# Attention and two MoE layers on one core: a four-operation weight decoder, diagonals and sums moved to other engines, a split transpose, loads in thirds, and a 32-byte filler

## The chip, the core and the metric

The kernel runs on one core of a Trainium2 chip. The metric is the device time of one execution in microseconds (us); the number before the change is the median of three runs. One further execution was recorded by the hardware profiler, and every row below comes from it. The engines are named as in the profile: PE is the tensor engine's matmul stream, PEld its weight loads, DVE the vector engine, ACT the scalar engine, POOL the GpSimd engine, SP the engine whose queue issues the DMAs.

## The reference

The three stages follow one another, in fp32 (the inputs are 4 x 8 x 576 x 64 for q, k and v; the weights w1, w2 and w3, w_out of the MoE layers have 512 x 768, 768 x 512, 512 x 2048 and 2048 x 512 elements):

```python
scores = q @ k.T / 8 + bias            # bias[h] = relu(log1p(|i-j|)/log1p(max(i,1)) * w1 + b1) @ w2
attn = exp(scores - max(scores)); attn = attn / (sum(attn) + 1e-9)
x = attn @ v                           # to 2304 tokens x 512
h = max(x @ m.w1, x @ m.w2, x @ m.w3)  # 2304 x 768, relu included through the maxima
x = h @ m.w_out                        # 2304 x 512
g = elu(x @ m2.w_in)                   # 2304 x 2048
out = g @ m2.w_out                     # 2304 x 512
```

The weights of the MoE layers arrive as float64 bits (two int32 words for each number) and are turned into float32 on the chip. Both MoE layers compute in a split form: a number is a high part in fp32r plus a low part in fp32r, so that each product takes three matmuls (high by high, high by low, low by high).

## The kernel before

**Prologue (0 to 56 us).** The bias table of all heads is computed with matmuls and written to scratch tiles `scr` in memory. Its last writes end in the first steps of the attention.

**Attention (56 to about 343 us).** There are 16 head pairs n, each with 5 query blocks c, so 80 steps s. Blocks 0 to 3 have 128 queries and both heads; block 4 holds the 64 queries that are left of both heads in one tile, so it has one of everything where the others have two ("one-head step"). A step does this: `unit_qk` (L222, PE) writes the scores of a head into PB[h]; `scores` (L230, DVE) adds the bias tile b_t, scales, stores e_t in SBUF and takes the row minimum; `expo` (L235, ACT) takes the exponential with its sum; `recip` (L240 and L241, DVE) makes 1/(sum + 1e-9); `diag` (L249, POOL, one operation for each head) multiplies a 64 x 64 identity by it, to dg_t; `trans` (L252, PE) multiplies 64 x 64 blocks of e_t by that diagonal into TQ, which transposes and normalises them; `tails` (L252 too, with output pb) does so for the last 64 keys, into columns of PB; `evac` and `evac_tails` (helper lines L75 on ACT, L77 on DVE) copy TQ and the tails to p; `pv` (L319, L323, L327, PE) multiplies by v into the two banks XO[0] and XO[1]. After blocks 1 and 4, `x_copy` (L341, ACT) copies XO[0] to xf, `x_sum` (L345, DVE) adds XO[1], and `x_hi` (L73) and `x_lo` (L81) on POOL split the result into the token tiles xh and xl, which hold all 2304 tokens.

The order in each engine's queue is written by hand: every piece has a key `s + OFF[name]`, and the pieces are issued in order of the key. OFF = qk0 0.0, qk1 0.01, t0 (`scores` of head 0) 0.02, t1 0.03, pump 0.32, ns (`recip`) 1.025, tr 2.10, tl 2.20, evt 2.311, ev0 2.385, ev1 2.387: step s computes scores, while the transposes are those of step s-2. Between t0 and t1 of a step the DVE thus runs the `recip` of the step before. PB[0] is written by `tails` and read by `scores` of head 0: the tails at 2.20 of step s-2 come after t0 of step s, and have to wait until it has read PB[0]. TQ and XO are of two banks each and PB is of two, so no step has a second set.

One `pump` in each step of four out of five runs a piece of the weight decoder (`decoder`, L420 to L430): DVE masks the exponent, ACT changes its bias (L422, with the constant tile `rebias`), DVE shifts and masks, twice combines, and merges (five DVE operations of 512 columns for a tile of 128 x 512 weights). 56 tiles are decoded in all, 14 of them in the attention. Then the split (ACT and POOL) and a store to memory. `load_kq` (L96) fetches q and k of the next pair (864 KB in one DMA), `load_v` (L100) its v, `fetch` (L371) raw weights, `load_b` (L109, L114) the bias tiles after each four pairs; all through SP's queue.

**First MoE layer (343 to 626 us)**: L526 is the matmul of `moe1_mm` (1296 of 128 x 128 by 384 columns, the moving operand being xh or xl), L620 that of `moe1_out` (432 of 384 columns, moving hh or hl). **Second (626 to 1008 us)**: L696 is that of `prod` (1020 of 384 columns, moving xh, xl or the sums tt), L740 that of `moe2_out` (864 of 512 columns, moving the weight tiles w_t, with gh or gl as weights). 94 matmuls of the first layer run already in the last steps of the attention.

**Addresses.** Within a partition every tile of these two layers and of the attention begins 32 bytes past a multiple of 64 (w_t at 17056, xh at 155360, xl at 192224, gh at 41632, hh at 107680), because the tile `rebias` of 4 bytes takes up 32 bytes ahead of them on the left side, and on the right side ident2 and the token tiles add up so. The blocks that a matmul streams are at multiples of 1536 or 512 bytes within the tiles, so each moving row begins 32 bytes past a multiple of 64 as well.

## Time and profile before

| what | value |
|---|---|
| median of three runs | 1013.38 us (1012.16 to 1016.56) |
| the profiled execution's own time | 1010.22 us |
| its span on the core | 1008.4 us |
| mean granted clock of PE | 0.997 of full speed |
| busy: PE, PEld, DVE, ACT, POOL | 977.4, 869.2, 692.1, 526.1, 341.7 us |
| share of PE in the chain of work that ended last | 91% |
| memory traffic | 150.78 MB read, 48.37 MB written |

The profile is read by stages here, since the stages have different limits: a mean over the span hides that PE has idle time in the attention only. The busy time of PE includes time in which a matmul is drawn out by its neighbours, so a row of the timeline gives the start and the drawn-out length of a group of instructions, and the distance between starts is what counts.

### The profile page before, as it was taken

How to read it: one execution, taken by the hardware profiler on the slowest of the kernel's cores; microseconds unless marked ns; L12 is line 12 of the kernel's file. 1: busy time of each engine (PE TensorE's matmuls, PEld its weight loads, DVE VectorE, ACT ScalarE, POOL GpSimd, SP SyncE). 2: the span in 40 equal slices, each digit the busy share in tenths (PEclk: the TensorE clock that was granted, in tenths of full speed). 3: DMA queues.
4: the chain of work that ended last, by engine and by line, in shares of the span. 5: the costliest groups of instructions: out<-in, count | busy, mean ns of one | idle time of the engine just before them, and what ended most of it. 6: DMA issues, size and time to landing. Idle time of an engine off the chain costs nothing.

```text
span 1008.4 us, 28525 instructions
## 1 busy us (share of the span) xinstructions
PE 977.4 (97%) x11748; PEld 869.2 (86%) x11748; DVE 692.1 (69%) x1428; ACT 526.1 (52%) x1087; POOL 341.7 (34%) x419
## 2 busy tenths in 40 slices
PE   7979899999999999999999999999999999999998
PEld 4447777778887899999999999998998989988996
DVE  7967778788886699887887862835574355743342
ACT  8967777777775233333333331644445344453443
POOL 0013344344343354534553550323232132321222
PEclk9989999999999999999999999999999999999999
DMA  7842724645532356879886981355657556575553
GB/s 259 291 172 85 247 94 157 205 163 187 176 127 79 134 187 215 308 234 341 321 282 236 328 298 47 116 189 175 199 192 252 191 171 204 188 258 185 176 197 105
DMA packets 65905, 201.00 MB, mean 199 GB/s; under 512 B 7024, under 2 KB 14832, under 8 KB 65776
## 3 DMA queue, kind: packets, MB, share of 16 engines
q1 hardware_dynamic: 65776, 199.18, 57.6%
q8 instruction: 93, 1.52, 0.6%
q14 instruction: 36, 0.29, 0.1%
HBM read 150.78 MB, written 48.37 MB: 197 GB/s over the span
## 4 chain that ended last, share of the span: by engine, by line
PE 91%; DVE 6%; issue 1%; DMA 1%; ACT 0%; SPq 0%; POOL 0%; DVEq 0%; POOLq 0%; ACTq 0%
PE xo L696 18%; PE pb L740 13%; PE pb L526 12%; PE tq L740 6%; PE tq L252 6%; PE xo L319 6%; PE xo L526 5%; PE tq L526 5%; PE pb L222 5%; PE pb L620 4%; PE pb L183 3%; PE pbb L183 2%; DVE e_t L230 2%; PE xo L620 2%; PE tq L620 2%
## 5 line engine op out<-in xcount | busy, mean ns | idle before, releaser
L81 POOL TENSOR_TENSOR gl<-t_t,gh 128x384 fp32r<-128x384 f32 x96 | 108.7, 1142 | 286.3 <-ACT gh L75 286.3
L235 ACT ACTIVATE e_t<-e_t,st_t 128x576 f32<-128x576 f32 x144 | 111.4, 773 | 58.6 <-DVE st_t L240 56.1
L230 DVE CUSTOM_DVE_ANT_0 e_t<-pb,b_t 128x576 f32<-128x576 f32 x144 | 107.7, 749 | 32.7 <-PE pb L222 32.5
L249 POOL TENSOR_SCALAR dg_t<-ident,st_t 128x64 f32<-128x64 f32 x144 | 48.1, 348 | 212.7 <-DVE st_t L241 93.2
L740 PE MATMUL pb<-w_t,gh 128*128 128x512 f32 x384 | 119.3, 392 | 0.0
L526 PE MATMUL pb<-xh,w_t 128*128 128x384 f32 x448 | 116.8, 336 | 0.0
L252 PEld LDWEIGHTS tq<-dg_t,e_t 64*64 64x64 f32 x4608 | 96.6, 136 | 22.7 <-issue 7.7
L252 PE MATMUL tq<-dg_t,e_t 64*64 64x64 f32 x4608 | 97.8, 222 | 10.9 <-issue 5.3
L696 PE MATMUL xo<-tt,w_t 128*128 128x384 f32 x528 | 107.4, 338 | 0.0
L718 ACT ACTIVATE t_t<-c_t 128x384 f32<-128x384 f32 x96 | 50.0, 521 | 103.4 <-DVE c_t L709 95.6
L222 PE MATMUL pb<-kq_t 64*64 64x288 f32 x1152 | 98.6, 413 | 3.8 <-issue 1.3
L696 PEld LDWEIGHTS xo<-tt,w_t 128*128 128x128 f32 x528 | 95.0, 188 | 7.7 <-issue 0.3
L696 PE MATMUL xo<-xh,w_t 128*128 128x384 f32 x328 | 94.6, 335 | 0.0
L319 PE MATMUL xo<-p,tv_t 64*64 64x320 f32 (+1 forms) x1024 | 85.4, 408 | 1.6 <-issue 1.2
L526 PEld LDWEIGHTS pb<-xh,w_t 128*128 128x128 f32 x448 | 81.1, 188 | 0.5 <-issue 0.4
L740 PEld LDWEIGHTS pb<-w_t,gh 128*128 128x128 f32 x384 | 70.5, 188 | 6.6
L740 PE MATMUL pb<-w_t,gl 128*128 128x512 f32 x192 | 75.5, 393 | 0.0
L526 PE MATMUL pb<-xl,w_t 128*128 128x384 f32 x224 | 75.3, 336 | 0.0
L75 ACT ACTIVATE p<-tq 128x512 f32<-128x512 f32 (+1 forms) x128 | 62.8, 528 | 16.4 <-PE tq L252 15.2
L222 PEld LDWEIGHTS pb<-kq_t 64*64 64x64 f32 x1152 | 50.9, 133 | 22.9 <-DVE p L77 4.4
L75 ACT ACTIVATE gh<-t_t 128x384 fp32r<-128x384 f32 x96 | 48.6, 519 | 33.4 <-DVE t_t L726 33.4
L696 PEld LDWEIGHTS xo<-xh,w_t 128*128 128x128 f32 x328 | 60.2, 188 | 3.0
(131 smaller groups left out, 2198.1 us busy)
## 6 DMA issues: line engine op xcount, KB each, us to landing
w_t<-scw_w SPq DMA_DIRECT2D x90, 512.0 KB, 4.4
w_t<-scw_wi SPq DMA_DIRECT2D x74, 512.0 KB, 4.2
kq_t<-tkq SPq DMA_DIRECT2D x16, 864.0 KB, 5.4
scw_wi<-sp SPq DMA_DIRECT2D x26, 512.0 KB, 4.7
scw_w<-sp SPq DMA_DIRECT2D x22, 512.0 KB, 5.5
raw<-wo SPq DMA_DIRECT2D x22, 512.0 KB, 3.7
scr<-o_t SPq DMA_DIRECT2D x36, 288.0 KB, 3.9
raw<-wm SPq DMA_DIRECT2D x18, 512.0 KB, 4.1
```

Source lines behind the costliest of these rows:

```text
L75: nc.scalar.activation(dst, src, AF.Copy)
L81: e.tensor_tensor(out=dst, in0=src, in1=hi.bitcast(F32), op=ALU.subtract)
L183: mm(p[32 * a4:32 * a4 + 32, 224 + 288 * hf:512 + 288 * hf], w28, FT[A, a4][:, 288 * hf:288 * hf + 288], start=True, stop=True)
L222: mm(PB[h][H64[g], 224 + 288 * r:512 + 288 * r], t[H64[r], 576 + 576 * a + q0:640 + 576 * a + q0], t[H64[r], 288 * a:288 * a + 288], start ...
L230: nc.vector.tensor_tensor_reduce(out=E[s][:, 576 * h:576 * h + 576], in0=PB[h][:, 224:800], in1=BT[n // 4, c, h], op0=ALU.add, op1=ALU.min ...
L235: nc.scalar.activation(e, e, AF.Exp, bias=st[:, h:h + 1], scale=-1.0, accum_out=st[:, 2 + h:3 + h])
L252: mm(dst, E[s][H64[g], k0:k0 + 64], DG[s][H64[g], h % nheads(s)], start=True, stop=True)
L319: mm(XO[g][H64[h], 0:w], v[H64[g], 128 * k + 64 * h:128 * k + 64 * h + 64], ps[0][H64[g], 4 * h + k, :], start=(k == 0), stop=(k == 3 and ...
L526: mm(ps[blk][:, 0:NB], wt[:, ks], xt[:, kk, t0:t0 + NB], start=(j == 0), stop=(j == 11))
L620: mm(ps[blk][:, 0:NB], WO[0][:, kk, wt, ms], xt[:, bs], start=(j == 0), stop=(j == 3 * NM1 - 1))
L696: mm(ps, w[wt][:, ks], b[xt][:, kk], start=(start and j == 0), stop=(stop and j == 5), skip_group_check=True)
L740: mm(acc[t], g[:, ts], w[k], start=(f == 0 and i == 0 and j == 0), stop=(f == NU - 1 and i == 1 and j == 2))
```

## The change

- **Decoder.** `magnitude` takes the absolute value of the high words as floats on ACT, one tile ahead; DVE then clamps it (max and min with two constants), shifts it left by three, and merges sign and low bits in two operations: four DVE operations instead of five, the number of pumps for a tile stays five. The tile `rebias` is gone.
- **Diagonals.** One DVE operation for both heads (L247 of the new file), right behind the reciprocal, in place of one or two on POOL.
- **Sums.** ACT copies both banks of XO to two tiles xf; POOL adds them.
- **Evacuation.** EVD has 3 beside 0 and 2: in block 3 the second half of TQ is copied by DVE and no longer by ACT.
- **Transposes.** `trans` is called for one head at a time, and the tails come between the two.
- **Loads.** q and k of the next pair come as three DMAs of 288 KB, at steps 1.2, 2.2 and 3.2 of a pair instead of one at 0.2; v one step later.
- **Addresses.** A tile of 32 bytes, `align`, is reserved beside xh and xl. With it and without `rebias` all the tiles named above begin at a multiple of 64 (w_t 17024, xh 155328, xl 192192, gh 41600, hh 107648). The tiles of the prologue stay where they were.

```diff
-OFF = {"qk0": 0.0, "qk1": 0.01, "t0": 0.02, "ns": 1.025, "dg": 1.026, "t1": 0.03, "tr": 2.10, "tl": 2.20, "evt": 2.311,
+OFF = {"qk0": 0.0, "qk1": 0.01, "t0": 0.02, "ns": 1.025, "t1": 0.03, "tr0": 2.10, "tl": 2.11, "tr1": 2.12, "evt": 2.311,
        "pump": 0.32, "ev0": 2.385, "ev1": 2.387, "ex0": 0.38, "ex1": 0.40}
-EVD = {0, 2}
+EVD = {0, 2, 3}
-    rebias = const.tile([128, 1], F32, name="rebias")
-    nc.vector.memset(rebias, -896.0 * 2.0 ** 23)
+    def load_kq(n, i=None):
+        if not i:
+            KQ[n] = kq.tile([128, 1728], F32, tag="kq", name="kq_t")
+        cs = slice(576 * i, 576 * i + 576) if i is not None else slice(0, 1728)
+        nc.sync.dma_start(KQ[n][:, cs], tkq[n][:, cs])
     XL = xp.tile([128, NP, NT], F32R, name="xl")
+    xp.tile([128, 8], F32, name="align")
         nc.vector.reciprocal(st[:, 6:6 + nh], st[:, 4:4 + nh])
-        for h in range(nh):
-            nc.gpsimd.tensor_scalar(DG[s][:, h], ident2, ST[s][:, 6 + h:7 + h], 1.0, op0=ALU.mult, op1=ALU.mult)
+        nc.vector.tensor_tensor(out=d[:, 0:nh], in0=ident2.unsqueeze(1).to_broadcast([128, nh, 64]),
+                                in1=st[:, 6:6 + nh].unsqueeze(2).to_broadcast([128, nh, 64]), op=ALU.mult)
-        XF[s] = tp.tile([128, 320], F32, tag="xf", name="xf", bufs=1)[:, 0:w]
-        nc.scalar.activation(XF[s], XO[0][:, 0:w], AF.Copy)
+        XF[s] = [tp.tile([128, 320], F32, tag=f"xf{i}", name="xf", bufs=1)[:, 0:w] for i in range(2)]
+        for i in range(2):
+            nc.scalar.activation(XF[s][i], XO[i][:, 0:w], AF.Copy)
-        nc.vector.tensor_tensor(out=XF[s], in0=XO[1][:, 0:w], in1=XF[s], op=ALU.add)
+        nc.gpsimd.tensor_tensor(out=XF[s][0], in0=XF[s][0], in1=XF[s].pop(), op=ALU.add)
+    def magnitude(i):
+        if i < len(DQ):
+            MAG[i] = wpre.tile([128, 512], F32, tag="x", name="x_t", bufs=2)
+            nc.scalar.activation(MAG[i], RAW[DQ[i]][:, :, 1].bitcast(F32), AF.Abs)
-            nc.vector.tensor_scalar(x, hi, 0x7FF00000, None, op0=ALU.bitwise_and)
+            x = MAG.pop(i)
+            nc.vector.tensor_scalar(x, x, LEAST, MOST, op0=ALU.max, op1=ALU.min)
             yield
-            nc.scalar.activation(x, x, AF.Relu, bias=rebias, scale=8.0)
-            nc.vector.tensor_scalar(t, hi, 3, 0x7FFFF8, op0=ALU.logical_shift_left, op1=ALU.bitwise_and)
+            nc.vector.tensor_scalar(t, x.bitcast(I32), 3, 0x3FFFFFF8, op0=ALU.logical_shift_left, op1=ALU.bitwise_and)
             yield
-            nc.vector.scalar_tensor_tensor(out=t, in0=hi, scalar=-0x80000000, in1=t, op0=ALU.bitwise_and, op1=ALU.bitwise_or)
+            nc.vector.scalar_tensor_tensor(out=t, in0=hi, scalar=-0x40000000, in1=t, op0=ALU.bitwise_and, op1=ALU.bitwise_or)
+            magnitude(i + 1)
             yield
             nc.vector.scalar_tensor_tensor(out=t, in0=lo, scalar=29, in1=t, op0=ALU.logical_shift_right, op1=ALU.bitwise_or)
             yield
             fetch()
-            nc.vector.tensor_tensor(out=t, in0=t, in1=x, op=ALU.bitwise_or)
-        at(5 * n + 0.2, load_kq, n + 1)
-        at(5 * n + 6.2, load_v, n + 1)
+        for i in range(3):
+            at(5 * n + 1.2 + i, load_kq, n + 1, i)
+        at(5 * n + 7.2, load_v, n + 1)
```

The order on PE, in a one-head step of the attention of before: tq are the two banks of TQ, pb_99 is PB[0], xo the banks of XO, and the rows of L252 with output tq go on to 16.

```order
L222 MATMUL pb_99<-kq_t 64x288 x4
L252 MATMUL tq_859<-dg_t,e_t 64x64 x2
L252 MATMUL tq_860<-dg_t,e_t 64x64 x2
...
L252 MATMUL pb_99<-dg_t,e_t 64x64 x4
L323 MATMUL xo_861<-p_3043,tv_t 64x256
L323 MATMUL xo_862<-p_3043,tv_t 64x256
L327 MATMUL xo_861<-p_3185,tv_t 64x64 x2
```

And in the same step of the changed kernel, where pb_97 is PB[0] and L251 is the transpose (8 rows of it ahead of the tails and 8 behind):

```order
L224 MATMUL pb_97<-kq_t 64x288 x4
L251 MATMUL tq_858<-dg_t,e_t 64x64 x2
L251 MATMUL tq_859<-dg_t,e_t 64x64 x2
...
L251 MATMUL pb_97<-dg_t,e_t 64x64 x4
L251 MATMUL tq_858<-dg_t,e_t 64x64 x2
L251 MATMUL tq_859<-dg_t,e_t 64x64 x2
...
L323 MATMUL xo_860<-p_3046,tv_t 64x256
```

The tails' four matmuls moved ahead of the second head's transposes, which now stand behind whatever the tails wait for.

The order on DVE at the same kind of place, in a two-head step with a sum, of before (L230 is `scores`, of head 0 from pb_99 and of head 1 from pb_100; L77 the evacuations, L420 the decoder's first operation):

```order
L230 ISA e_t,st_t<-pb_99,b_t 128x576
L230 ISA st_t 128x1
L240 TENSOR_SCALAR st_t<-st_t 128x2
L241 RECIPROCAL st_t<-st_t 128x2
L345 TENSOR_TENSOR xf<-xo_862,xf 128x256
L230 ISA e_t,st_t<-pb_100,b_t 128x576
L230 ISA st_t 128x1
L77 COPY p_1221<-pb_99 128x128
L420 TENSOR_SCALAR x_t<-raw 128x512
```

And of the changed kernel (L232 is `scores`, L244 and L245 the reciprocal, L247 the diagonals, L76 the evacuations):

```order
L232 ISA e_t,st_t<-pb_97,b_t 128x576
L232 ISA st_t 128x1
L244 TENSOR_SCALAR st_t<-st_t 128x2
L245 RECIPROCAL st_t<-st_t 128x2
L247 TENSOR_TENSOR dg_t<-ident_862,st_t 128x128
L232 ISA e_t,st_t<-pb_98,b_t 128x576
L232 ISA st_t 128x1
L76 COPY p_1216<-pb_97 128x128
L429 TENSOR_SCALAR x_t<-x_t 128x512
```

Between the two scores the sum of XO went out, and the diagonals came in, in every step.


## Rows read from the trace of the kernel before

**Rows 1.** Busy time by stage: PE, PEld, DVE, ACT, POOL, with instruction counts; clock, DMA share, GB/s.

```profile
0.00:56.00 56.00, 50.02 (x588) 24.63 (x592) 47.91 (x114) 51.49 (x73) 1.02 (x7) 1.00 0.74 271
56.00:343.20 287.20, 266.86 (x7649) 221.58 (x7649) 222.88 (x670) 201.84 (x480) 109.70 (x223) 0.99 0.45 152
343.20:626.14 282.94, 282.94 (x1634) 282.94 (x1633) 224.91 (x333) 100.97 (x190) 122.30 (x94) 1.00 0.72 253
626.14:1008.00 381.86, 377.56 (x1885) 340.04 (x1883) 196.38 (x312) 171.78 (x344) 108.68 (x96) 1.00 0.56 185
```

**Rows 2.** The chain that ended last, both MoE layers: start, us, what, matmuls.

```profile
351.52 4.16 PE tq L526 x24
...
652.03 1.38 PE pb L740 x6
...
672.54 1.39 PE tq L740 x6
```

**Rows 3.** Timeline of PE, attention: start, length, line, output and inputs, count.

```profile
267.03 0.75 PE L222 MATMUL pb<-kq_t 64*64 64x288 f32 x8
267.52 1.20 PE L252 MATMUL tq<-dg_t,e_t 64*64 64x64 f32 x64
268.67 0.34 PE L252 MATMUL pb<-dg_t,e_t 64*64 64x64 f32 x8
...
269.43 1.20 PE L222 MATMUL pb<-kq_t 64*64 64x288 f32 x16
270.45 1.11 PE L252 MATMUL tq<-dg_t,e_t 64*64 64x64 f32 x64
271.38 0.30 PE L252 MATMUL pb<-dg_t,e_t 64*64 64x64 f32 x8
```

**Rows 4.** Timeline of DVE over the same steps; in brackets idle time and what ended it.

```profile
267.85 0.76 DVE L230 CUSTOM_DVE_ANT_0 e_t<-pb,b_t 128x576 f32<-128x576 f32 x1 [0.74 <-PE pb L222]
...
270.23 0.75 DVE L230 CUSTOM_DVE_ANT_0 e_t<-pb,b_t 128x576 f32<-128x576 f32 x1
```

**Rows 5.** Groups of DVE and POOL in the attention: busy, mean ns, idle before them and releaser.

```profile
L77 DVE COPY p<-tq 128x512 f32<-128x512 f32 x32 | 21.8, 682 | 0.0
...
L345 DVE TENSOR_TENSOR xf<-xo,xf 128x256 f32<-128x256 f32 (+1 forms) x32 | 14.0, 439 | 1.1 <-ACT xf L341 1.1
L241 DVE RECIPROCAL st_t<-st_t 128x2 f32<-128x2 f32 (+1 forms) x80 | 13.2, 165 | 2.7
...
L430 DVE TENSOR_TENSOR t_w<-t_w,x_t 128x512 int32<-128x512 int32 x14 | 11.3, 806 | 3.3 <-ACT x_t L422 3.2
...
L81 POOL TENSOR_TENSOR xl<-xf,xh 128x256 fp32r<-128x256 f32 (+1 forms) x32 | 30.6, 956 | 2.2
```

**Rows 6.** Timeline of DVE: a decoder operation with two inputs in SBUF.

```profile
257.28 1.25 DVE L427 SCALAR_TENSOR_TENSOR t_w<-raw,t_w 128x512 int32<-128x512 int32 x1
```

**Rows 7.** Timeline of POOL at the same moment.

```profile
257.12 0.87 POOL L81 TENSOR_TENSOR xl<-xf,xh 128x320 fp32r<-128x320 f32 x1
```

**Rows 8.** Timeline of SP's queue: start, us to issue, line, tiles.

```profile
119.90 0.34 SPq L96 DMA_DIRECT2D kq_t<-tkq  x1
```

**Rows 9.** The chain, attention: the longest stretches in which PE had no recorded releaser.

```profile
120.31 1.72 issue
125.40 1.19 issue
143.94 1.33 issue
...
210.64 1.15 issue
```

**Rows 10.** The chain at the attention's start.

```profile
58.77 3.58 DMA scr<-o_t
...
63.69 0.33 POOL dg_t L249
...
64.06 1.99 PE tq L252 x64
```

More of the change, by code (lines that the diff above doesn't have):

```diff
@@ L30 @@
 BIG = 3.0e38
-OFF = {"qk0": 0.0, "qk1": 0.01, "t0": 0.02, "ns": 1.025, "dg": 1.026, "t1": 0.03, "tr": 2.10, "tl": 2.20, "evt": 2.311,
+LEAST, MOST = (float(np.array(b, np.uint32).view(np.float32)) for b in (896 << 20, 0x47EFFFFF))
+OFF = {"qk0": 0.0, "qk1": 0.01, "t0": 0.02, "ns": 1.025, "t1": 0.03, "tr0": 2.10, "tl": 2.11, "tr1": 2.12, "evt": 2.311,
        "pump": 0.32, "ev0": 2.385, "ev1": 2.387, "ex0": 0.38, "ex1": 0.40}
@@ L235, in expo, with diag @@
         nc.scalar.activation(e, e, AF.Exp, bias=st[:, h:h + 1], scale=-1.0, accum_out=st[:, 2 + h:3 + h])
-    def recip(s):
-        nh = 2 if steps[s][1] < 4 else 1
+    DG = {}
+    def diag(s):
+        nh = nheads(s)
         st = ST[s]
@@ L241, in recip @@
         nc.vector.reciprocal(st[:, 6:6 + nh], st[:, 4:4 + nh])
-    DG = {}
-    def diag(s):
-        nh = 2 if steps[s][1] < 4 else 1
-        DG[s] = sp.tile([128, 2, 64], F32, tag="dg", name="dg_t", bufs=3)
-        for h in range(nh):
-            nc.gpsimd.tensor_scalar(DG[s][:, h], ident2, ST[s][:, 6 + h:7 + h], 1.0, op0=ALU.mult, op1=ALU.mult)
+        d = DG[s] = sp.tile([128, 2, 64], F32, tag="dg", name="dg_t", bufs=3)
+        nc.vector.tensor_tensor(out=d[:, 0:nh], in0=ident2.unsqueeze(1).to_broadcast([128, nh, 64]),
+                                in1=st[:, 6:6 + nh].unsqueeze(2).to_broadcast([128, nh, 64]), op=ALU.mult)
     def flip(dst, s, g, h, k0):
@@ L271, in tails, with trans @@
                 flip(x[h][0:64], s, h, 0, 512)
-    def trans(s):
+    def trans(s, h):
         n, c = steps[s]
-        if c == 0:
+        if h:
+            pass
+        elif c == 0:
             PT[n, 0] = [tp.tile([128, 8, 256], F32, tag="pa", name="p0", bufs=1)]
@@ L278, in trans @@
             PT[n, 1] = [tp.tile([128, 8, 320], F32, tag="pc", name="p1", bufs=1)]
-        if c in (0, 2):
+        if h == 0 and c in (0, 2):
             PT[n, c // 2].append(tp.tile([128, 256], F32, tag="p3", name="p3", bufs=3))
-        elif c == 4:
+        elif h == 0 and c == 4:
             PT[n, 1].append(tp.tile([64, 128], F32, tag="p4", name="p4", bufs=1))
-        for h in range(nheads(s)):
-            for k in range(4):
-                for g in range(2):
-                    for kh in range(2):
-                        col = 256 * h + 64 * k
-                        flip(TQ[g][H64[kh], col:col + 64], s, g, h, 576 * h + 128 * k + 64 * kh)
+        for k in range(4):
+            for g in range(2):
+                for kh in range(2):
+                    col = 256 * h + 64 * k
+                    flip(TQ[g][H64[kh], col:col + 64], s, g, h, 576 * h + 128 * k + 64 * kh)
     def evac(s, g):
@@ L339, in x_copy @@
         w = x_where(s)[2]
-        XF[s] = tp.tile([128, 320], F32, tag="xf", name="xf", bufs=1)[:, 0:w]
-        nc.scalar.activation(XF[s], XO[0][:, 0:w], AF.Copy)
+        XF[s] = [tp.tile([128, 320], F32, tag=f"xf{i}", name="xf", bufs=1)[:, 0:w] for i in range(2)]
+        for i in range(2):
+            nc.scalar.activation(XF[s][i], XO[i][:, 0:w], AF.Copy)
     def x_sum(s):
-        w = x_where(s)[2]
-        nc.vector.tensor_tensor(out=XF[s], in0=XO[1][:, 0:w], in1=XF[s], op=ALU.add)
+        nc.gpsimd.tensor_tensor(out=XF[s][0], in0=XF[s][0], in1=XF[s].pop(), op=ALU.add)
+        XF[s] = XF[s][0]
     def x_hi(s):
@@ L403, in split @@
                 fn()
+    MAG = {}
+    def magnitude(i):
+        if i < len(DQ):
+            MAG[i] = wpre.tile([128, 512], F32, tag="x", name="x_t", bufs=2)
+            nc.scalar.activation(MAG[i], RAW[DQ[i]][:, :, 1].bitcast(F32), AF.Abs)
     def decoder():
+        magnitude(0)
         for i, key in enumerate(DQ):
@@ L559, in fused_kernel @@
             at(o["ex1"], expo, s, 1)
-        at(o["ns"], recip, s)
-        at(o["dg"], diag, s)
-        at(o["tr"], trans, s)
+        at(o["ns"], diag, s)
+        at(o["tr0"], trans, s, 0)
+        if c < 4:
+            at(o["tr1"], trans, s, 1)
         at(o["tl"], tails, s)
```

4 lines of the change are left out of this document (removed).

## The prediction

> **What bounds the kernel now.** I read the busy time by stage first, since a mean over the span mixes stages with different limits. In the two MoE layers the tensor engine is busy for 282.94 of 282.94 us and for 377.56 of 381.86 us [rows 1]; DVE, the next engine, has 224.91 and 196.38 us, and the DMA share is 0.72 and 0.56. In the chain of waits these stages are nothing but rows of PE, one behind the other. So only what changes the distance between two matmuls can change these 665 us; work that DVE saves there (the decoder's fifth operation, 42 tiles) is worth nothing. The attention is different: 266.86 us of PE in 287.20, DVE 222.88, and both drawn out by waits for each other. There an edit acts by its place in the loop.
>
> The distance between matmuls comes from the chain [rows 2]: 24 of 384 columns take 4.16 us, so one takes 173.3 ns, which at 2.4 GHz (granted clock 1.00 in these stages) is 416 cycles, 32 more than its columns. Six of 512 columns take 1.38 to 1.39 us, 230 to 232 ns, or 552 to 556 cycles, 40 or more above 512. The two overheads differ by 8 cycles or a little more for 128 more columns, that is for 512 bytes more of each partition's moving row: one cycle for each 64 bytes, on top of 8 for each matmul (384 columns are 24 units of 64 bytes, 512 are 32). In the kernel before every one of these rows begins 32 bytes past a multiple of 64. After the change every one begins at a multiple of 64.
>
> **The change, part by part.**
>
> *The addresses.* If the extra cycle for each 64 bytes comes from rows that straddle these units, it goes: 24 cycles or 10.0 ns for each matmul of 384 columns, 32 cycles or 13.3 ns for each of 512. There are 1296 + 432 + 1020 = 2748 of the first and 864 of the second, nearly all in the two stages in which PE hardly waits, so the sum is 27.5 + 11.5 = 39.0 us off. If the extra cycle belongs to streaming fp32r at all, it stays and the part is worth nothing. No row shows a stream of these matmuls at a multiple of 64, so both ends stand: 0 and 39, and 51 us at most (2748 x 13.3 + 864 x 16.7 ns, if the 8 cycles went as well). A loss is excluded, since a row that begins at the start of a unit touches no more units than one that begins in its middle. I take 39, on the count alone: an overhead that grows by one for each 64 bytes, in a kernel where each row is cut by 64-byte units at an odd place, is what double accesses would give, and a stream that could not keep its rate at any address would be the odder design. I give it a little over one half. What is late next if it goes: DVE would need 224.91 us in about 266 in the first MoE layer, and the DMA share would be 0.77, so PE stays the bound.
>
> The Trainium skill (TensorE: Matmul & The Clock Gate, section Back-to-back issue gap) gives a gap of N/2.4 + 2.5 ns at full clock, which is 162.5 and 215.8 ns here, with no term for the address. The trace of before disagrees with it by 10.8 and about 14 ns; by the skill's gap the two layers would be some 42 us shorter than they are, and nothing on the page says for which operands or addresses it was measured.
>
> *The tails between the two heads' transposes.* The tails write PB[0], which DVE's scores of head 0 must have read. In the one-head step, the scores' operation runs from 267.85 to 268.61 [rows 4] and the tails start at 268.67 [rows 3], 0.06 us behind its end: they waited. In the two-head step it ends at 270.98 and the tails start at 271.38: a slack of 0.40. The 64 transposes of a step take 0.93 us from 270.45 to 271.38, so a head's share is 0.465 us, and the tails now come that much earlier. In the one-head step they wait all of it, with the second head's transposes behind them on PE: +0.465 us, 16 times, 7.4 us. In the two-head steps 0.465 less 0.40 plus the 0.06 that a release takes gives a wait of about 0.12 us, 64 times, 7.9 us at most, and 0 where DVE's loop sets the step anyway. I take a tenth of it, as in these steps DVE's row shows no idle time before the scores (the bracket at 270.23 is empty). Together +8, from 0 to 15.
>
> *DVE's loop.* For a head pair it loses two sums of 0.439 us and 14/16 of a decoder operation of 0.806 [rows 5], 1.58 us. It gains five diagonals and one evacuation in block 3 of 0.682 us. A diagonal (128 columns, two operands in SBUF) has no row; the reciprocal of 2 columns takes 0.165 and the decoder's merge of 512 columns 0.806 on average, so 0.165 to 0.81; I take 0.2, near the small one (128 columns lie nearer to 2 than to 512), and 1.0 for five. The balance is 0.1 us against DVE, and the work is moved from the two steps with a sum (0.24 us shorter each) to the others. The two lighter steps are those in which DVE has most to do, so I take -2 us for 16 pairs, from -8 (those two count alone) to +10 (five diagonals of 0.3).
>
> *Meetings of DVE and POOL.* A decoder operation on DVE that began 0.16 us behind a POOL subtraction took 1.25 us [rows 6, 7], 0.44 above the mean of the merge, which has as many columns. The sums now come to POOL (32 of about 0.96, as its subtractions of the same size) and the diagonals go from POOL (48 us) to DVE, in reach of such a meeting. POOL's subtractions of xl, 30.6 us [rows 5], and its sums, as much again, are 61 of 287 us. If that share of the 80 diagonals, 17, lost 0.44 us each, that is 7.5; what DVE loses is on the chain only where DVE sets the step. I take +2, from 0 to 8.
>
> The Trainium skill (SBUF — State Buffer, section Who interferes with whom) calls the shared port pair of the two engines an exclusive lock. By it a diagonal with both inputs in SBUF waits until POOL's operation is over, and the two tiles of a sum cost POOL the same wait; that is the upper end, 8 in place of 2, and the sum would be 984.
>
> *The thirds.* PE stands still in the attention without a recorded releaser; the four longest such stretches are 1.72, 1.19, 1.33 and 1.15 us [rows 9], 5.4 us in all. One begins at 120.31, right behind the issue of the 864 KB of q and k at 119.90 [rows 8], and the others have that load and v's near them too. Smaller loads, set apart from v, should leave shorter ones. I take -5, from -5.4 to 0.
>
> *The start.* DVE's copies of the identity wait for the last bias write (58.77, 3.58 us), then come the diagonals and at 64.06 the first transposes [rows 10]. Now the first diagonals on DVE, and so the scores of the next steps behind them in DVE's queue, wait for these copies too, which before had run ahead. One score is 0.75 us: +1, from 0.5 to 3.
>
> *At no cost:* ACT's copies of the second XO bank, of the sum's size (32 x 0.439 = 14 us), and the magnitudes, which replace as many operations of ACT: it is at 201.84 of 287.20 us [rows 1]. If that cover were gone, 14 us.
>
> **The sum.** Attention: +8 - 2 + 2 - 5 + 1 = +4. MoE layers: -39. From the profiled execution's own 1010.2 us this makes 975; the median of the runs shown is 3.2 us above that execution, so 978 (the +3.2 stands for what one execution differs from the median). With the terms at their ends (attention -13 to +22, but not all at once: -10 to +18; addresses -51 to -39) this case by itself runs from 960 to 993.
>
> **The rivals.** *The pitch stays, and the attention nearly balances:* 1013.4 + 4 = 1017, between 1009 and 1018. For it: nothing but the arithmetic of two row lengths speaks for the addresses. *Slower:* the pitch stays, and the wait of the tails is on the path in every step: 15.3 us for the tails, -2 for DVE, +4 for meetings, -2 for the loads, +1, in sum +16: 1029. It decides when more than half of the two-head steps are bound by PE, so that 0.12 us each counts; the scores' idle time of 0.74 us in the one-head step [rows 4] shows DVE waiting for PE in such places. *Faster without the addresses:* the stretches of issue go (-5.4), the two lighter steps decide for DVE (-8), the tails cost only the 7.4 of the one-head steps: 1013.4 - 6 = 1007. *The addresses count for one half:* only the rows of 512 columns, or only those of one side, gain: -12 to -27, with +4, 990 to 1006.
>
> **How the numbers follow.** Addresses in full 0.48, in part 0.04, faster without them 0.06, balanced 0.21, slower 0.21. A measurement of this kernel can tell about 0.5%, 5 us, from no change; so faster by more is 0.48 + 0.04 + 0.06 = 0.58, within it 0.21, slower 0.21. The likeliest case is 978, with its own range 960 to 993. The range that should hold 8 in 10 goes from 964 (below it the 8 cycles would have to go too) to 1023, which leaves out the upper part of the slower case.
>
> **What would show it.** The groups of 24 matmuls in the chain at 3.92 us and those of six at 1.30 instead of 4.16 and 1.38 if the addresses count, unchanged if not; this is the step on which all hangs. The first MoE layer in about 266 us and the second in about 360. In the attention: the tails 0.06 us behind the scores' end in one-head steps, with 2.87 us from one qk to the next in place of the 2.40 from 267.03 to 269.43 [rows 3]; a diagonal's row at about 0.2 us; fewer and shorter stretches of issue; the attention's length at 287 + 4. I am wrong if the rows' lengths stay, or if PE then waits for weights or for memory in the MoE layers.

## The result, and the profile after

The changed kernel takes 1025.73 us (median of four, 1024.63 to 1027.57) where the kernel before took 1012.77 beside it: a ratio of 1.0129, with a 95% interval of 1.0089 to 1.0170. It is 1.3% slower, clear of the interval, and outside the range forecast. The profiled execution took 1027.57 us with a span of 1025.7; that of the kernel before took 1010.22, so the two traces are 17.3 us apart where the medians are 13.0.

The stages of the changed kernel's trace come first, with the columns of [rows 1]:

```profile
0.00:56.00 56.00, 50.21 (x592) 24.38 (x596) 48.00 (x114) 51.43 (x73) 1.02 (x7) 1.00 0.75 271
56.00:359.90 303.90, 274.48 (x7646) 206.72 (x7639) 241.18 (x720) 207.97 (x497) 82.24 (x110) 0.99 0.44 144
359.90:642.80 282.90, 282.90 (x1634) 282.90 (x1633) 193.28 (x290) 97.99 (x192) 122.18 (x95) 1.00 0.72 253
642.80:1025.70 382.90, 378.05 (x1888) 340.79 (x1886) 196.40 (x312) 171.82 (x344) 108.69 (x96) 1.00 0.56 184
```

The two MoE layers take 282.90 and 382.90 us, as before (282.94 and 381.86 in [rows 1]). Nearly all of the difference between the two traces is in the attention: 303.90 us for 287.20. There DVE's busy time rose from 222.88 to 241.18 us although a decoder operation and the sums were taken from it, and POOL's fell from 109.70 to 82.24. The first MoE layer shows the decoder's saving, DVE at 193.28 instead of 224.91 us, with no effect on the length, as the prediction said of a stage that PE fills.

The chain that ended last, first MoE layer, answers [rows 2]:

```profile
402.11 4.16 PE tq L534 x24
...
669.34 1.38 PE pb L750 x6
```

24 matmuls of 384 columns still take 4.16 us, and six of 512 columns (L750) still take 1.38. Every moving row begins at a multiple of 64 bytes now, and both lengths are what they were.

Next the groups of DVE in the attention, columns as in [rows 5]:

```profile
L76 DVE COPY p<-tq 128x512 f32<-128x512 f32 x48 | 32.7, 682 | 2.4 <-PE tq L251 1.7 <-PE xo L327 0.5
L247 DVE TENSOR_TENSOR dg_t<-ident,st_t 128x128 f32<-128x128 f32 (+1 forms) x80 | 25.0, 313 | 2.7
...
L244 DVE TENSOR_SCALAR st_t<-st_t 128x2 f32<-128x2 f32 (+1 forms) x80 | 22.2, 277 | 0.3 <-ACT e_t L237 0.3
...
L433 DVE SCALAR_TENSOR_TENSOR t_w<-raw,t_w 128x512 int32<-128x512 int32 x14 | 11.0, 785 | 0.1
```

The same group as L244 in the kernel before, the addition of 1e-9 to one or two columns:

```profile
L240 DVE TENSOR_SCALAR st_t<-st_t 128x2 f32<-128x2 f32 (+1 forms) x80 | 12.8, 160 | 0.3 <-ACT e_t L235 0.3
```

So the diagonals cost DVE 25.0 us, not 16; the evacuations of TQ grew by 16 operations, 10.9 us; and an operation that nobody had touched grew by 9.4 us. Against this stand 14.0 us of sums and 15.4 us of decoder (five groups of 55.5 us together before, four of 40.1 now). How the long ones of L244 come about is seen by putting the timeline of DVE beside that of POOL. DVE of the changed kernel (start, length):

```profile
273.19 0.63 DVE L244 TENSOR_SCALAR st_t<-st_t 128x2 f32<-128x2 f32 x1
276.82 1.08 DVE L244 TENSOR_SCALAR st_t<-st_t 128x2 f32<-128x2 f32 x1
...
283.57 0.15 DVE L244 TENSOR_SCALAR st_t<-st_t 128x1 f32<-128x1 f32 x1
```

and POOL:

```profile
273.06 0.73 POOL L345 TENSOR_TENSOR xf<-xf 128x256 f32<-128x256 f32 x1 [4.78 <-ACT xf L342]
...
276.60 1.28 POOL L80 TENSOR_TENSOR sp<-t_w,sp 128x512 fp32r<-128x512 f32 x1 [1.50 <-ACT sp L74]
...
283.44 0.87 POOL L345 TENSOR_TENSOR xf<-xf 128x320 f32<-128x320 f32 x1 [5.55 <-ACT xf L342]
```

POOL's operation of 276.60, a part of the weight split, ends at 277.88, DVE's two columns at 277.90. With a sum on POOL from 273.06 to 273.79, the L244 of 273.19 took 0.63 us and ended at 273.82: the small operation ends when POOL's does. Of the 80, 16 are longer than 0.25 us and make up the 9.4 us: 14 meet a sum of 256 columns, two the weight split. The last rows show what does not wait: in one-head steps L244 has one column, and 14 of these 16 began inside a sum of 320 columns and took 0.15 us as ever.

The chain in the attention shows what this does. One head pair of the changed kernel, in order of time (start, us, what):

```profile
282.88 0.76 DVE e_t L232
...
283.95 0.44 DVE dg_t L247
284.38 0.67 DVE e_t L232
...
285.06 0.20 DVE p L76
285.26 1.08 DVE t_w L433
286.35 0.61 DVE p L76
...
290.70 0.63 DVE st_t L244
...
300.33 0.76 DVE e_t L232
```

The first row and the last are the same place of two head pairs in a row, 17.45 us apart. For the first 4 us the chain runs through one DVE operation after the other, with the diagonal among them, and the held-up L244 comes behind; much of what is left out is PE. In the kernel before the same place stands at 255.09 and at 270.23 [rows 4], 15.14 us apart, but that is the shortest of its pairs: of 15 such distances the middle one is 16.27 us before and 17.40 after, and together they are 244.4 and 260.6 us. What the chain is made of from 56 to 330 us, before and after:

```profile
by line: PE tq L252 22.2%; PE xo L319 20.5%; PE pb L222 18.0%; DVE e_t L230 7.8%; issue 4.7%; PE pb L252 4.7%; DVE p L77 4.1%; DVE t_w L423 3.9%; PE pb L526 3.2%; PE xo L323 3.0%; DVE t_w L425 1.3%; DMA scr<-o_t 1.3%; DVE xf L345 1.2%; DVE 
```
```profile
by line: PE pb L224 17.2%; DVE e_t L232 17.2%; PE tq L251 14.0%; PE xo L319 13.1%; DVE p L76 5.7%; issue 5.3%; PE pb L251 5.1%; PE xo L323 3.9%; DVE st_t L244 3.6%; DVE dg_t L247 3.1%; DVE x_t L429 2.0%; DVE t_w L433 1.9%; DVE st_t L245 1.9
```

The groups of DVE named there went from 18% to 35% of the chain, those of PE from 72% to 53%. A large part of the bound went from PE to DVE, and the two share it now.

### The profile page after: what moved, and what is told of

Read it like the earlier page. It is cut to its first block, busy times and chain, and to the rows that moved or that the text cites. A ratio compares the mean times of both kernels' runs of the same rounds, so it can differ in the third digit from the quotient of the medians.

```text
span 1025.7 us, 28378 instructions
## 1 busy us (share of the span) xinstructions
PE 985.6 (96%) x11748; PEld 854.8 (83%) x11748; DVE 678.9 (66%) x1435; ACT 529.2 (52%) x1103; POOL 314.1 (31%) x307
## 4 chain that ended last, share of the span: by engine, by line
PE 85%; DVE 11%; DMA 2%; issue 2%; ACT 1%; SPq 0%; DVEq 0%; ACTq 0%
PE xo L706 17%; PE pb L750 13%; PE pb L534 11%; PE tq L750 6%; PE xo L534 5%; PE tq L534 5%; DVE e_t L232 5%; PE pb L224 5%; PE xo L319 4%; PE tq L251 4%; PE pb L630 4%; PE pb L184 2%; PE xo L630 2%; PE tq L630 2%; PE pbb L184 2%; DVE p L76 2%
## 5 line engine op out<-in xcount | busy, mean ns | idle before, releaser
L232 DVE CUSTOM_DVE_ANT_0 e_t<-pb,b_t 128x576 f32<-128x576 f32 x144 | 108.0, 751 | 32.1 <-PE pb L224 31.9
L750 PE MATMUL pb<-w_t,gh 128*128 128x512 f32 x384 | 119.3, 392 | 0.0
L251 PEld LDWEIGHTS tq<-dg_t,e_t 64*64 64x64 f32 x4608 | 97.8, 136 | 22.2 <-DVE p L76 6.1
L251 PE MATMUL tq<-dg_t,e_t 64*64 64x64 f32 x4608 | 104.3, 221 | 6.5 <-DVE p L76 4.0
L345 POOL TENSOR_TENSOR xf<-xf 128x256 f32<-128x256 f32 (+1 forms) x32 | 25.6, 799 | 260.2 <-ACT xf L342 260.2
L224 PE MATMUL pb<-kq_t 64*64 64x288 f32 x1152 | 91.8, 416 | 10.0 <-DVE st_t L232 6.5
L411 ACT ACTIVATE x_t<-raw 128x512 f32<-128x512 f32 x56 | 37.6, 671 | 97.5 <-DMA raw<-win 47.4
L319 PE MATMUL xo<-p,tv_t 64*64 64x320 f32 (+1 forms) x1024 | 79.0, 406 | 2.8 <-issue 2.8
L224 PEld LDWEIGHTS pb<-kq_t 64*64 64x64 f32 x1152 | 42.9, 133 | 40.8 <-DVE p L76 20.9
L750 PEld LDWEIGHTS pb<-w_t,gh 128*128 128x128 f32 x384 | 70.5, 188 | 6.6
L750 PE MATMUL pb<-w_t,gl 128*128 128x512 f32 x192 | 75.5, 393 | 0.0
```

Source lines behind the costliest of these rows:

```text
L224: mm(PB[h][H64[g], 224 + 288 * r:512 + 288 * r], t[H64[r], 576 + 576 * a + q0:640 + 576 * a + q0], t[H64[r], 288 * a:288 * a + 288], start ...
L232: nc.vector.tensor_tensor_reduce(out=E[s][:, 576 * h:576 * h + 576], in0=PB[h][:, 224:800], in1=BT[n // 4, c, h], op0=ALU.add, op1=ALU.min ...
L251: mm(dst, E[s][H64[g], k0:k0 + 64], DG[s][H64[g], h % nheads(s)], start=True, stop=True)
L319: mm(XO[g][H64[h], 0:w], v[H64[g], 128 * k + 64 * h:128 * k + 64 * h + 64], ps[0][H64[g], 4 * h + k, :], start=(k == 0), stop=(k == 3 and ...
L750: mm(acc[t], g[:, ts], w[k], start=(f == 0 and i == 0 and j == 0), stop=(f == NU - 1 and i == 1 and j == 2))
```

## The experiments

Names that begin with u_ undo something in the changed kernel, those with b_ do one part alone in the kernel before. Ratios are to the kernel before on the same chip, with 95% intervals; the changed kernel's is 1.0129 (1.0089 to 1.0170).

| run | edit | us | ratio |
|---|---|---|---|
| u_sum_dve | sums back on DVE | 1032.59 | 1.0230 (1.0195 to 1.0265) |
| u_diag_pool | diagonals back on POOL | 1021.65 | 1.0122 (1.0084 to 1.0161) |
| u_unsplit | tails last again | 1024.49 | 1.0141 (1.0102 to 1.0179) |
| u_no_filler | no filler | 1033.68 | 1.0247 (1.0204 to 1.0289) |
| u_diag_unsplit | diagonals on POOL and tails last | 1015.93 | 1.0049 (1.0026 to 1.0071) |
| u_kq_whole | q and k in one load | 1033.23 | 1.0233 (1.0218 to 1.0248) |
| u_duk | diagonals on POOL, tails last, q and k in one load | 1012.90 | 1.0020 (0.9998 to 1.0042) |
| u_evd02 | evacuation of block 3 on ACT | 1023.65 | 1.0109 (1.0083 to 1.0136) |
| b_split | only the split transposes | 1019.10 | 1.0094 (1.0061 to 1.0126) |
| b_diag | only the diagonals on DVE | 1021.50 | 1.0129 (1.0089 to 1.0169) |
| b_thirds | only the loads in thirds | 1015.08 | 1.0050 (1.0035 to 1.0066) |
| b_decoder | only the new decoder | 1011.32 | 1.0010 (0.9991 to 1.0029) |
| b_sum | only the sums on POOL | 1012.69 | 1.0022 (0.9990 to 1.0053) |
| b_diag_sum | diagonals on DVE, sums on POOL | 1023.71 | 1.0107 (1.0058 to 1.0157) |
| b_filler | only the filler | 1014.02 | 1.0034 (1.0008 to 1.0060) |
| b_filler96 | a filler of 96 bytes | 1011.42 | 0.9991 (0.9971 to 1.0010) |

### One part undone: neither the diagonals nor the tails by themselves

u_sum_dve puts `x_copy` and `x_sum` back:

```diff
-        for i in range(2):
-            nc.scalar.activation(XF[s][i], XO[i][:, 0:w], AF.Copy)
+        nc.scalar.activation(XF[s], XO[0][:, 0:w], AF.Copy)
-        nc.gpsimd.tensor_tensor(out=XF[s][0], in0=XF[s][0], in1=XF[s].pop(), op=ALU.add)
+        nc.vector.tensor_tensor(out=XF[s], in0=XO[1][:, 0:w], in1=XF[s], op=ALU.add)
```

> The changed kernel with the sum of the two XO banks back on DVE (one copy on ACT, the addition between reciprocal and second scores), all else changed. In the trace of the changed kernel the operation that adds 1e-9 (L244, 128x2) takes 0.277 us on average and up to 1.08, where it took 0.160 before, and its long ones end with a POOL operation that reads two tiles. Theory LOCK (DVE is held up by POOL's sums): L244 goes back to about 0.16 except beside the weight split, 9.4 us of DVE go, 14.0 of sums come, of which about 0.35 us each showed in the loop: 1022 us, and the diagonals fall from 0.313 to 0.29. Theory LOAD (only DVE's busy time counts): +14.0 - 9.4, so 1026 to 1030. Theory TAILS (the transposes' new order made the time): no change, 1025.

1032.59 us, 7 above the changed kernel by the medians, 10 by the ratios, and above all three forecasts. The group of L244 fell, as LOCK said (the window cuts off three steps):

```profile
L247 DVE TENSOR_TENSOR dg_t<-ident,st_t 128x128 f32<-128x128 f32 (+1 forms) x77 | 21.4, 279 | 2.6
L244 DVE TENSOR_SCALAR st_t<-st_t 128x2 f32<-128x2 f32 (+1 forms) x77 | 14.4, 187 | 0.5 <-ACT e_t L237 0.5
```

But the time went the other way. The hold-up is real and is not the main cost: the 14 us of sums on DVE are dearer than the hold-up that they avoid.

u_diag_pool:

```diff
-        nc.vector.tensor_tensor(out=d[:, 0:nh], in0=ident2.unsqueeze(1).to_broadcast([128, nh, 64]),
-                                in1=st[:, 6:6 + nh].unsqueeze(2).to_broadcast([128, nh, 64]), op=ALU.mult)
+        for h in range(nh):
+            nc.gpsimd.tensor_scalar(d[:, h], ident2, st[:, 6 + h:7 + h], 1.0, op0=ALU.mult, op1=ALU.mult)
```

> The changed kernel with the diagonals back on POOL, one operation for each head, all else changed. DVE loses 80 operations of 0.313 us, 25.0 us. Theory LOAD: they stand in the loop of scores, reciprocal, second scores in every step, so nearly all of it comes back: 1003 to 1008. Theory LOCK: the reciprocal's first operation is still held by POOL's sums, and the diagonals now queue behind the sums on POOL and so come late: 1012 to 1022. Theory TAILS: 1018 to 1025, since PE then waits for the tails instead.

1021.65 us: 4 us below the changed kernel by the medians, under 1 by the ratios. LOAD, which wanted 17 to 22, fell; LOCK and TAILS both allowed this time. Its PE timeline (columns as in [rows 3]) tells why:

```profile
290.28 0.64 PE L251 MATMUL tq<-dg_t,e_t 64*64 64x64 f32 x32
291.46 0.34 PE L251 MATMUL pb<-dg_t,e_t 64*64 64x64 f32 x8 [0.54 <-DVE st_t L232]
291.62 0.59 PE L251 MATMUL tq<-dg_t,e_t 64*64 64x64 f32 x28
```

With DVE relieved, the tails stand between the two heads' transposes and wait for the scores. L244 is at 13.4 us for 80 there, although the sums are on POOL: with the diagonals in POOL's queue no sum ran beside it.

u_unsplit:

```diff
-"tr0": 2.10, "tl": 2.11, "tr1": 2.12,
+"tr0": 2.10, "tl": 2.20, "tr1": 2.12,
```

> The changed kernel with the tails behind both heads' transposes again (key 2.20 in place of 2.11), all else changed. Theory TAILS: the 7.4 us of the one-head steps and up to 7.9 of the others go: 1011 to 1018. Theories LOAD and LOCK: DVE sets the steps, PE has time to wait, so 1023 to 1026; the evacuation of the tails, which stands in DVE's queue, comes later by half a transpose (0.47 us) and may even cost: up to 1030.

1024.49 us, within 2 us of the changed kernel: TAILS fell as the only cause.

### Two parts undone, and each alone: two walls

u_diag_unsplit makes the last two edits together.

> The changed kernel with both undone, the diagonals back on POOL and the tails behind both heads' transposes. Each alone moved the time by 4 us or less. Theory TWO WALLS: with diagonals on DVE the loop of DVE sets the steps and hides what the tails' place costs; with them on POOL, PE sets the steps and its chain shows a wait for the scores ahead of the tails twice in each head pair. Then both together give back far more than the sum of the two: 1003 to 1011 where the changed kernel has 1025. Theory ADD (the two are small costs by themselves and the time sits elsewhere, in the loads or the decoder): 1018 to 1021.

1015.93 us, 10 below the changed kernel (8 by the ratios), where the two edits apart gave 4 and 1 (1 and -1 by the ratios). That is the mark of two walls of about the same height: DVE's loop and PE's wait for the tails. The time lies between the two forecasts, 1003 to 1011 and 1018 to 1021; some 4 us above the kernel before remained.

b_split is the kernel before with `trans` called for one head at a time and the keys of the changed kernel; b_diag is the kernel before with the changed kernel's `diag`:

```diff
-        at(o["tr"], trans, s)
+        at(o["tr0"], trans, s, 0)
+        if c < 4:
+            at(o["tr1"], trans, s, 1)
```

> The kernel before with only the transposes split and the tails between the heads; diagonals on POOL, sums and decoder as before. Theory TWO WALLS: here PE sets the steps, so the tails' wait shows in full: 7.4 us of the one-head steps and more from others, 8 to 16 us above the kernel before. Theory ADD: 0 to 3 above it, as undoing it in the changed kernel gave 1.

1019.10 us, 7.4 above by the medians and 9.5 by the ratio. Its PE waits (what waited, for what: us, times, longest) from 56 to 330 us, and those of the kernel before:

```profile
PE pb L252 <- DVE st_t L230: 7.6, 21, 0.5
```
```profile
PE pb L252 <- DVE st_t L230: 1.3, 5, 0.6
```

The wait grew by 6.3 us and from 5 to 21 times. The one-head steps have 15 of the 21, at 0.42 us each in nearly all, 6.4 us in all, where the prediction had 0.465 and 7.4; the other six, of 0.2 us, are in two-head steps. The changed kernel's trace has this wait too, though undoing the split there gave back 1 us at most:

```profile
PE pb L251 <- DVE st_t L232: 6.4, 15, 0.4
```

> The kernel before with only the diagonals moved to DVE, in the order of the changed kernel; sums on DVE, decoder of five operations, tails last. Theory TWO WALLS: DVE gets 80 operations of about 0.3 us, 24 us, with nothing taken from it, in a loop that is already at its limit in the steps with a sum or a decoder operation: 14 to 24 us above the kernel before. Theory ADD: 3 to 5 above it.

1021.50 us, 9.8 above by the medians and 13.0 by the ratio, which is that of the whole change. It is less than the 14 to 24 of TWO WALLS and far more than the 3 to 5 of ADD. The prediction took 0.2 us for a diagonal; here it is this, with the small addition beside it:

```profile
L245 DVE TENSOR_TENSOR dg_t<-ident,st_t 128x128 f32<-128x128 f32 (+1 forms) x80 | 22.3, 279 | 2.7
...
L242 DVE TENSOR_SCALAR st_t<-st_t 128x2 f32<-128x2 f32 (+1 forms) x80 | 14.8, 185 | 0.3 <-ACT e_t L235 0.3
```

So this one edit puts 24.3 us more on DVE. DVE's idle time before the scores, from 56 to 330 us, fell from 32.7 to 23.3 us, so that part was filled in; the other 14.9 us are near the 10 to 13 that the kernel lost. Scores on DVE are 18.7% of the chain there, for 7.8% before. No run has the diagonals on DVE at another place of its queue, so what the place between the two scores costs by itself is open.

### The sums and the evacuation

b_sum is the kernel before with the sums on POOL; b_diag_sum adds the diagonals on DVE; u_evd02 is `EVD = {0, 2}` in the changed kernel.

> The kernel before with only the sums of the two XO banks moved: two copies on ACT, the addition on POOL. The diagonals stay on POOL, in its queue ahead of the sum that has the next key, so a sum starts only when the reciprocal of that step is done. Theory LOCK: then the operation that adds 1e-9 (L240) stays at 0.16 us, and DVE loses 14 us in the two steps where it has most to do: 2 to 6 us below the kernel before. Theory LOAD: the same, since PE sets these steps: within 2 us.

1012.69 us, no difference: 14 us off DVE bought nothing, as LOAD said. LOCK's 0.16 us for L240 fell: it was at 217 ns. Of its 80 operations 14 were long, all beside POOL's subtractions to xl, which now come behind the sums.

> The kernel before with the diagonals on DVE and the sums on POOL; decoder, tails and loads as before. With the diagonals alone on DVE the kernel stood 13 us above the kernel before, the operation that adds 1e-9 at 0.185 us, the diagonal at 0.279. Theory LOCK: nothing on POOL waits for the reciprocal now, so its sums run into it: that operation at 0.26 us or more and the diagonals at 0.31, 5 to 9 us of DVE lost again, of the 14 that the sums gave; 8 to 13 us above the kernel before. Theory LOAD: 14 us of DVE gone, 3 to 7 us above it, the operation at 0.185.

1023.71 us, where b_diag had 1021.50: inside LOCK's 8 to 13 above the kernel before. The busy time of the two groups rose, as LOCK said:

```profile
L245 DVE TENSOR_TENSOR dg_t<-ident,st_t 128x128 f32<-128x128 f32 (+1 forms) x80 | 26.0, 325 | 2.7
L242 DVE TENSOR_SCALAR st_t<-st_t 128x2 f32<-128x2 f32 (+1 forms) x80 | 20.5, 257 | 0.3 <-ACT e_t L235 0.3
```

DVE lost 14 us of sums and got 9.4 of hold-ups (3.7 on the diagonals, 5.7 on the addition). The time is the same within the intervals. In u_sum_dve the same move, seen the other way, was worth 7 to 10 us; why it is worth nothing here is open.

> The changed kernel with the second half of block 3's transposes evacuated by ACT again. DVE loses 16 operations of 0.682 us. Where DVE sets the step, as its chain shows in the changed kernel: 5 to 11 us below the changed kernel. If DVE's idle time hid it: the same within 2.

1023.65 us, 2 below the changed kernel and inside the intervals: less than the 5 expected from 10.9 us of DVE work. So these copies are hardly on the path, and the changed kernel is not bound by DVE's busy time as such.

### The loads

b_thirds is the kernel before with three loads of 288 KB, u_kq_whole the changed kernel with one of 864, u_duk the changed kernel with three parts undone (diagonals, tails, loads):

```diff
-        for i in range(3):
-            at(5 * n + 1.2 + i, load_kq, n + 1, i)
-        at(5 * n + 7.2, load_v, n + 1)
+        at(5 * n + 0.2, load_kq, n + 1)
+        at(5 * n + 6.2, load_v, n + 1)
```

> The kernel before with only the loads in thirds. My prediction took 5 us off for it. Theory LOADS: 2 to 6 us above the kernel before, with pairs 3, 7 and 11 longer, where the bias tiles are loaded. Prediction: 5 us below it, with fewer stretches without a releaser on PE.

1015.08 us, 4 to 5 above the kernel before. The prediction had 5 below. The waits of PE without a releaser, at its transposes, from 56 to 330 us, of b_thirds:

```profile
PE tq L254 <- issue: 12.0, 8, 3.4
```

and of the kernel before:

```profile
PE tq L252 <- issue: 5.3, 7, 1.7
```

The longest, of 3.4 us, begins at 184.96, in the eighth pair. SP's queue just before it:

```profile
178.72 0.42 SPq L98 DMA_DIRECT2D kq_t<-tkq  x1
179.61 2.39 SPq L111 DMA_DIRECT2D b_t<-scr  x2
182.62 1.09 SPq L116 DMA_DIRECT2D b_t<-scr  x2
```

The pairs that load the bias tiles now have q, k and v moved into the same steps, and the stretches got longer rather than shorter. Pairs 3, 7 and 11, counted from 0, grew by 1.4, 2.7 and 2.0 us against the kernel before, as LOADS said; that is more than the whole difference.

> The changed kernel with three parts undone: diagonals on POOL, tails last, and q and k of the next pair in one load at the old place (v too). What stays is the decoder of four operations, the sums on POOL, the third block's evacuation on DVE, the addresses. With the first two undone the kernel stood 4 us above the kernel before, and its trace had 13.6 us of stretches without a releaser on PE where the kernel before had 9.5. Theory LOADS (the thirds come into the way of the bias tiles in every fourth pair and cost 4 us): 1 to 6 us below the kernel before, since DVE has 13 us less to do. Theory NO LOADS: 4 us above the kernel before as with two parts undone.

1012.90 us, 3 below u_diag_unsplit with intervals that overlap, and no different from the kernel before.

> The changed kernel with q and k in one load at the old place, all else changed. Theory LOADS: 3 to 6 us below the changed kernel. Theory TWO WALLS alone: DVE sets the steps and hides the loads: the same within 2 us.

1033.23 us: 7.5 us slower than the changed kernel by the medians, 10 by the ratios, against both theories. In the changed kernel the thirds help. Its waits without a releaser show where:

```profile
PE xo L317 <- issue: 6.3, 3, 2.6
...
PE pb L222 <- issue: 2.7, 2, 1.8
...
PE tq L249 <- issue: 1.5, 4, 0.5
```

10.5 us in the group, where the changed kernel has 5.8. So the sign of this edit depends on the rest of the kernel; on what in it is open. What holds PE in such a stretch has no releaser in the trace, and no run isolated it.

### The decoder

> The kernel before with only the decoder of four operations (the unused constant tile stays, so no address changes). DVE loses 14 operations of 0.806 us in the attention and 42 later, where PE is full. If DVE's loop sets the steps: 3 to 8 us below the kernel before; if PE does: the same within 2 us. DVE's load in the first MoE layer falls from 225 to about 193 us with no effect on the time by all theories.

1011.32 us, no difference: as forecast for steps that PE sets, with the two layers behind full on PE.

### The addresses

u_no_filler drops one line from the changed kernel, b_filler puts it into the kernel before, b_filler96 a tile of 96 bytes:

```diff
-    xp.tile([128, 8], F32, name="align")
```

> The changed kernel without the filler of 32 bytes: xh and xl begin 32 bytes past a multiple of 64 again, all other tiles at a multiple. The changed kernel's matmuls keep the distance of before (24 of 384 columns in 4.16 us), so by all theories the time stays, 1023 to 1028, and so do the 4.16 us for rows of xh and xl. If 32 bytes did count for something, the rows of xh would be slower than those of hh: 27 us on 2300 matmuls by the arithmetic of the prediction, 1050.

1033.68 us, a ratio of 1.0247: against what all theories said, it is slower than the changed kernel. Its chain has the first layer's matmuls at a new distance, and the output product (L629) at the old one:

```profile
401.59 4.24 PE tq L533 x24
```

4.24 us for 24 is 176.7 ns or 424 cycles, 8 more than the 416 of the changed kernel, at a granted clock of 1.00. 1296 matmuls of the first layer and 492 of the second read xh or xl, so this is worth 1788 x 3.3 ns = 6 us of the 8 by the medians (12 by the ratios).

The slower distance is no creation of this edit. In the second layer of the kernel before, six matmuls that stream xh and xl (first row) and six that stream tt (second row) take:

```profile
653.41 1.04 PE xo L696 x6
...
655.83 1.06 PE xo L696 x6
```

1.06 us for six is 176.7 ns again. Of 82 such groups with tt 61 took 1.06 us or more, and none of 64 with xh and xl; the changed kernel has the same picture. Without the filler the groups with xh and xl take 1.06 as well.

> The kernel before with only the filler of 32 bytes: xh and xl at a multiple of 64, the weight tiles w_t still 32 bytes past one. In the changed kernel without the filler it was the other way round, and 24 matmuls of xh or xl with w_t took 4.24 us in place of 4.16, those of hh with the output weights stayed at 6.24 for 36. Theory RELATIVE (what counts is whether the moving row and the weights have the same place within 64 bytes): 4.24 here too, 2000 to 2300 matmuls by 3.3 ns, 7 us above the kernel before. Theory ROW (a moving row at a multiple of 64 is the better one by itself): 4.16 or less, so the kernel before or up to 7 us below it.

1014.02 us over ten runs, 1009.7 to 1019.2: 2 to 3 above the kernel before, between the two theories. The trace has both distances in one execution, with the same addresses modulo 64 and a granted clock of 1.00, the slower up to 417 us, the faster after the first output product:

```profile
353.48 4.24 PE tq L527 x24
...
446.20 4.16 PE tq L527 x24
```

> The kernel before with 96 bytes of filler: xh and xl begin at a multiple of 128, the weights w_t 32 bytes past one, so the moving rows lie 96 bytes ahead of the weights' place, modulo 128; the changed kernel without its filler had the same difference of 96 with xh at 96 and w_t at 0, and was slow there, while differences of 64 (before and after), 0 (the sums tt of the second layer) and 32 (32 bytes of filler in the kernel before) were not. Theory DIFFERENCE: 24 matmuls of xh with w_t take 4.24 us, 7 us above the kernel before. Theory PLACE (a moving row 32 bytes past a multiple of 64 with weights at a multiple is slow): 4.16, no change.

1011.42 us, with 4.16 us throughout the first layer. DIFFERENCE fell: a difference of 96 was slow in u_no_filler and is not here. The text above took the differences 0 (tt) and 32 (b_filler) for fast ones, and both were seen slow. PLACE forecast this run rightly, but does not cover the slow pass of b_filler nor the tt streams. What is shown: in the first layer these streams run at one of two distances, 416 or 424 cycles, held over a pass of some 75 us; dropping the filler puts the changed kernel's xh and xl streams on the slower one. What picks the distance is open.

## Why the prediction was wrong

**The addresses, -39 us.** This was the step that decided the number, and it failed. The two lengths were read rightly, but one cycle for each 64 bytes is a formula drawn from two lengths, and it gave no cause; the choice between the two causes rested on which design would be "odder". With every row at a multiple of 64 both lengths stayed as they were, 173.3 ns for 384 columns, and the two layers changed by 1 us, not 39. The kernel before could have warned: its groups with tt, begun at the same 32 bytes past a multiple of 64, take 424 cycles, 40 above their columns, about as many as the matmuls of 512 columns, so the overhead does not go by bytes there. What the overhead comes from is open. The gap that the prediction takes from the Trainium skill (TensorE: Matmul & The Clock Gate, section Back-to-back issue gap) is given there for an isolated matmul, not for a stream, so its distance from these rows speaks for neither cause. The filler is not worth nothing: without it the changed kernel is 8 to 12 us slower. It keeps a distance that the kernel before had already.

**The tails, +8.** Right in place and size for that part alone: 7.4 to 9.5 us, with 6.4 us of waits in the one-head steps. Wrong as a term of a sum: in the changed kernel undoing it moved the time by 1 us, because DVE's loop had become the longer one: the two edits had to be undone together to give 8 to 10 us.

**DVE's loop, -2.** The step that failed in the attention, which took 16.7 us more in the traces where +4 was forecast. The diagonal was sized at 0.2 us by its column count and takes 0.279 alone and 0.313 in the changed kernel. More than that, the forecast netted what DVE gave against what it got over a head pair, as if both had the same price. In the kernel before, what it gave bought nothing (0 to 2 us for the decoder operation and for the sums, each removed alone), since PE set the steps. This is not a matter of place alone: the sums stood between two scores as the diagonals do now. What it got cost 10 to 13 us when added alone, beyond the 9 us of idle time that it could fill.

**Meetings of DVE and POOL, +2.** The mechanism was right, the victim missed. It was priced on the diagonals alone. The addition of 1e-9 in front of them went from 12.8 to 22.2 us because nothing on POOL waited for the reciprocal any more. In the kernel before the diagonals on POOL kept its operations and DVE's apart, and no L240 was long; b_sum shows that they do not do so in every order. The Trainium skill (SBUF — State Buffer, section Who interferes with whom) speaks of an exclusive lock; the row of 1.08 us that ends 0.02 us behind POOL's operation agrees.

**The thirds, -5.** Wrong in sign on the kernel before (+4 to +5), right in sign on the changed one (7.5 to 10 us). The stretches were put down to the size of a load; b_thirds shows longer ones with smaller loads, in the pairs where the bias tiles come between them.

**The start, +1.** As forecast, PE waits there for scores that stand behind the first diagonals:

```profile
65.49 1.24 PE L224 MATMUL pb<-kq_t 64*64 64x288 f32 x8 [5.71 <-DVE st_t L232]
66.51 1.08 PE L251 MATMUL tq<-dg_t,e_t 64*64 64x64 f32 x32
```

The first transposes begin at 66.51 us where [rows 10] has 64.06: 2.4 us, inside the bounds of 0.5 to 3.

**The decoder in the MoE layers and ACT's copies at no cost.** As forecast. In the attention the decoder gave DVE 15.4 us back, not the 11.3 of one operation in each of 14 tiles.

**The rivals.** The slower rival gave 1029, near the time, by the wall that was not the upper one: it had PE's wait for the tails on the path and DVE's loop giving 2 us back, so that its nearness is luck. The range's upper end of 1023 left out the upper part of that case, and the time fell there. The parts alone add up to about 31 us (9.5, 13, 5, 2 and 1 by the ratios, the last two not clear of noise; the evacuation has no such run), the change costs 13: in the changed kernel the tails hide under DVE's loop (u_unsplit) and the thirds help (u_kq_whole).

No version that beats the kernel before came out of it: b_filler96, b_decoder and u_duk are level with it.

## What to carry to other kernels

Before netting work moved between engines, ask which engine sets the step: what is taken from the other one buys nothing, and what is given to it costs as soon as it has filled that engine's idle time. Here 14 us of sums off DVE bought nothing and 24 us of diagonals onto it cost 10 to 13. When two engines are within a few per cent of each other, undo suspects in pairs: undone singly, each of two walls looks innocent. An overhead that fits a neat formula says nothing about its cause until a row exists with the suspected cause changed; look through the trace at hand for rows that break the formula first.

## What the runs showed of the hardware that was not expected

- A DVE operation on two columns, in and out of SBUF, took up to 1.08 us where it takes 0.16 alone, and ended 0.02 us behind a POOL operation with two inputs. The same operation on one column took 0.15 us inside POOL's sum, 14 times of 14.
- Streams of fp32r matmuls of 384 columns ran at one of two distances, 173.3 or 176.7 ns, in the first layer over passes of some 75 us, in one execution both. With rows of xh at 32 past a multiple of 64 and weights at a multiple it was the slower in all of the layer, with both 32 past or both at a multiple the faster; but the streams of tt, at the same place as their weights too, ran mostly at the slower one.
- 24 matmuls of 384 columns take 4.16 us, 32 cycles for each above their columns, with moving rows 32 bytes past a multiple of 64 and with rows at one.
